# Local attention and a feed-forward layer: a tile of 128 queries split into two of 64 with 120 keys each

## The chip, the core and the metric

The kernel runs on one NeuronCore of a Trainium2 chip. The engines are TensorE (matmuls, written PE; its loads of the stationary operand are listed apart as PEld), VectorE (DVE), ScalarE (ACT), GpSimd (POOL) and SyncE (SP), which issues the DMAs. The metric is the device time of one execution in microseconds (us); lower is better.

## The reference

The attention of 4 batches of 768 tokens with 8 heads of 64 is followed by a feed-forward layer. Each query sees the keys closer than 16 positions to its own, and beside them 24 summary keys, one for each block of 32 tokens (the maximum of the block's keys, with the mean of its values):

```python
block, window = (32, 16)
nb = S // block                                   # 24
k_sum = k.reshape(B, H, nb, block, D).max(axis=3)
v_sum = v.reshape(B, H, nb, block, D).mean(axis=3)
mask_l = np.abs(pos[:, None] - pos[None, :]) < window
scores_s = scale * np.einsum('bhsd,bhnd->bhsn', q, k_sum) + np.log(block)
scores_all = np.concatenate([np.where(mask_l, scale * q @ k^T, -1e9), scores_s], axis=-1)
a = softmax(scores_all)
attn = np.matmul(a, np.concatenate([v, v_sum], axis=2))
# feed-forward on x = attn as (3072, 512)
h = x @ w_in                                      # (512, 2048)
out = (h * sigmoid(h)) @ w_out                    # (2048, 512)
```

Everything is f32. The time goes mostly into the feed-forward products.

## The kernel before

**Stages.** The 3072 tokens are 24 stages of 128 queries (`s`; six to a batch). A stage handles its 8 heads in four groups of two (`m = 4 s + g`). A query tile needs its own 128 keys, 15 on either side (the side block, 30 of 32 places) and the 24 summary keys: `NKEY` = 128 + 32 + 24 = 184.

**A head group (`job_a`).** TensorE multiplies queries and keys (L555; one block of instructions serves two head groups; the 64 rows of one head and the 64 of another are used side by side and write two PSUM banks). VectorE adds the mask and takes the maximum (L561), ScalarE makes the exponential and its sum (L564), VectorE the reciprocal (L568, L569), and one of three engines scales (L574, L576, L578). In batch 0 all this is f32: TensorE transposes the weights, the 128 own keys (L587) and the 56 others (L589), copies bring them back (L225, L229), and the products with v are f32 too (L619), a main block of 128 rows and a side block of 56. In batches 1 to 3 operands are split into a high and a low f16 part. The scores are three products (high by high, low by high, high by low), VectorE makes the low part of the weights (L602, four operations a head group), a DMA transposes them (L605), and the products with v (`job_c`, L634) are five terms for each of 8 heads, 40 matmuls of 128 columns a stage, two heads side by side in the two halves of the array's columns.

**v.** `job_mean` loads the six v tiles of batch 0 (L483), and a matmul with a matrix of 1/32 (`blocks`, L485) sums them into the 24 means. `job_vs` loads the side block (L501) and copies the means below it. `job_scale0` takes the maxima of v (L492). The two places for these tiles that lie in the weight buffers `wr` are given to the last weights later.

**Feed-forward (`job_f`).** Chunks of 256 tokens; for each of 16 slices of the hidden layer, L727 (chunk 0, f32) or L730 (f16, 12 matmuls) makes h, ScalarE the tanh (L744), VectorE the product (L745), and L735 or L738 multiplies by w_out. The weights are loaded in 32 pieces of 512 KB (L660), decoded by ScalarE and VectorE (L674, L670, L676), measured (L677) and after a common scale (`w_scale`) split (L683, L685). Chunk 0 uses them in f32, before the scale is known. It needs x of stages 0 and 1, which is copied by L225 and L229.

**Order.** Every operation is told to a planner (`Plan.op`) with a cost for each engine that may do it, its reads and writes, and a priority from the table `TUNE`. The planner fixes engine and order in advance; every engine then runs its instructions in that order. Where it sees TensorE wait early, it puts fillers (L316, L722), matmuls without use for the result. All loads go through SyncE's one queue.

Of the kernel before, what the change touches and what calls it, by code (L numbers as in the profile page):

```python
# [20 lines left out]
DM, DFF = 512, 2048  # L21
# [7 lines left out]
NSIDE = BLK  # L29
NLOC = P + NSIDE  # L30
NKEY = NLOC + NB
NS2 = NSIDE + NB
UW = 3 * P
# [4 lines left out]
NSTG = NT // P  # L38
NPAIR = NSTG * 4
# [179 lines left out]
def local_attn_ffn(ctx: ExitStack, tc: tile.TileContext, qkT, qF, kF, v, vR, w, out):  # L219
# [27 lines left out]
    blocks = const.tile([P, 11 * 4], F32, name="blocks")  # L247
    nc.vector.memset(blocks, 0.0)
    for j in range(4):
        nc.vector.memset(blocks[j * BLK:(j + 1) * BLK, 20 + j:21 + j], 1.0 / BLK)  # L250
# [3 lines left out]
    nc.vector.memset(masks[:, :, :NLOC], 0.0)  # L254
    nc.vector.memset(masks[:, :, NLOC:], math.log(BLK) / ISQ)
    for i in range(3):
        m = masks[:, i, :]
        nc.gpsimd.affine_select(out=m[:, :P], in_=m[:, :P], pattern=[[-1, P]], compare_op=ALU.is_ge, fill=NEG, base=HALO, channel_multiplier=1)
        nc.gpsimd.affine_select(out=m[:, :P], in_=m[:, :P], pattern=[[1, P]], compare_op=ALU.is_ge, fill=NEG, base=HALO, channel_multiplier=-1)
        if i == 0:  # L260
            nc.vector.memset(m[:, P:P + HALO], NEG)
        else:
            nc.gpsimd.affine_select(out=m[:, P:P + HALO], in_=m[:, P:P + HALO], pattern=[[1, HALO]], compare_op=ALU.is_ge, fill=NEG, base=0, channel_multiplier=-1)
        if i == 2:
            nc.vector.memset(m[:, P + HALO:NLOC], NEG)
# [7 lines left out]
    first = const.tile([P, max(NP * 2 * UW + 8 * DM, NTILE * 8 * NKEY)], F16, name="first")  # L273
    second = const.tile([P, 2 * max(8 * QW + 8 * NB, (NQ0 + NS0) * DM)], F16, name="second")
# [61 lines left out]
    def nudge(tag, *at):  # L336
        return NUDGE.get("_".join((tag,) + tuple(str(x) for x in at)), 0.0)
# [570 lines left out]
```

## Time and profile before

| | |
|---|---|
| median of 3 runs | 634.98 us (634.79 to 636.36) |
| the profiled execution | 634.78 us, its span 633.0 us |
| busy: PE, DVE, ACT, POOL | 625.0, 498.6, 400.7, 86.3 us |
| granted TensorE clock | 0.999 |
| DMA | 79.63 MB, 126 GB/s over the span |

The span is the time from the first to the last instruction of the program; 1.8 us lie around it. Busy time of TensorE counts overlapping matmuls once. A line of the timeline has start, length, engine, line of the code, operation, output and inputs, shape and count; a shape such as `128*64 128x128` is rows by columns of the stationary operand, and the moving operand. An f32 matmul stands as two records. A block is a run of matmuls of one line; its cost is the time from its start to the start of the block behind it, which contains the change of shape.

### The profile page before, as it was taken

How to read it: one execution, taken by the hardware profiler on the slowest of the kernel's cores; microseconds unless marked ns; L12 is line 12 of the kernel's file. 1: busy time of each engine (PE TensorE's matmuls, PEld its weight loads, DVE VectorE, ACT ScalarE, POOL GpSimd, SP SyncE). 2: the span in 40 equal slices, each digit the busy share in tenths (PEclk: the TensorE clock that was granted, in tenths of full speed). 3: DMA queues.
4: the chain of work that ended last, by engine and by line, in shares of the span. 5: the costliest groups of instructions: out<-in, count | busy, mean ns of one | idle time of the engine just before them, and what ended most of it. 6: DMA issues, size and time to landing. Idle time of an engine off the chain costs nothing.

```text
span 633.0 us, 13973 instructions
## 1 busy us (share of the span) xinstructions
PE 625.0 (99%) x5001; PEld 415.3 (66%) x5001; DVE 498.6 (79%) x1656; ACT 400.7 (63%) x1072; POOL 86.3 (14%) x125
## 2 busy tenths in 40 slices
PE   7999999999999999999999999999999999999997
PEld 4566666666666666666666666676666666666664
DVE  6899979977899785997989984998897968843332
ACT  3899969864885674665757674665765556533333
POOL 2311000130434100101003100001114104000000
PEclk9999999999999999999999999999999999999999
DMA  8999151222543593562553772454451523310000
GB/s 271 357 415 364 28 183 59 93 60 71 175 106 94 154 215 103 141 148 76 149 119 42 195 215 85 109 144 112 140 117 45 164 50 48 87 28 1 35 0 35
DMA packets 84455, 79.63 MB, mean 126 GB/s; under 512 B 60416, under 2 KB 66560, under 8 KB 84384
## 3 DMA queue, kind: packets, MB, share of 16 engines
q1 hardware_dynamic: 84384, 78.73, 44.0%
q8 instruction: 39, 0.64, 0.4%
q14 instruction: 32, 0.26, 0.1%
HBM read 56.49 MB, written 6.29 MB: 99 GB/s over the span
## 4 chain that ended last, share of the span: by engine, by line
PE 85%; DMA 5%; DVE 4%; ACT 3%; SPq 1%; issue 1%; ACTq 0%
PE bank L730 37%; PE bank L738 37%; PE bank L555 4%; DMA wr<-in_w_dram 4%; PE bank L634 4%; DVE wm L677 1%; PE bank L735 1%; DVE wr L676 1%; PE bank L619 1%; ACT wr L674 1%; ACT wr L670 1%; SPq L354 1%; DMA wr<-in_v_dram 1%; DMA raw<-in_qF_dram 1%; PE bank L727 1%
## 5 line engine op out<-in xcount | busy, mean ns | idle before, releaser
L730 PE MATMUL bank<-x,wr 128*128 128x256 f16 x2112 | 258.7, 273 | 0.0
L730 PEld LDWEIGHTS <-wr 128*128 128x128 f16 x2112 | 205.2, 98 | 57.0 <-issue 2.3
L738 PE MATMUL bank<-wr,gh 128*128 128x512 f16 x704 | 209.8, 380 | 0.0
L744 ACT ACTIVATE t<-bank,th 128x256 f32<-128x256 f32 x176 | 82.7, 470 | 119.2 <-PE bank L730 118.9
L745 DVE SCALAR_TENSOR_TENSOR t<-t,bank 128x256 f32<-128x256 f32 x192 | 79.5, 415 | 72.8 <-ACT t L744 72.0
L738 PE MATMUL bank<-wr,gl 128*128 128x512 f16 x352 | 133.4, 379 | 0.0
L747 ACT ACTIVATE gh<-t 128x256 f16<-128x256 f32 x176 | 72.3, 413 | 67.8 <-DVE t L745 60.1
L748 DVE SCALAR_TENSOR_TENSOR gl<-t,gh 128x256 f16<-128x256 f32 x176 | 80.8, 460 | 29.3 <-ACT gh L747 28.7
L738 PEld LDWEIGHTS <-gh 128*128 128x128 f16 x704 | 65.3, 98 | 48.2 <-issue 3.8
L564 ACT ACTIVATE e<-e,mx 128x184 f32<-128x184 f32 x192 | 83.5, 436 | 5.9 <-DVE mx L561 5.7
L602 DVE SCALAR_TENSOR_TENSOR first<-e,sum,first 128x128 f16<-128x128 f32 (+1 forms) x288 | 78.6, 333 | 0.3 <-POOL first L576 0.3
L738 PEld LDWEIGHTS <-gl 128*128 128x128 f16 x352 | 34.4, 98 | 41.6 <-DVE gl L748 0.2
L561 DVE CUSTOM_DVE_ANT_0 e<-bank,masks,qsc 128x184 f32<-128x184 f32 x144 | 52.1, 401 | 2.5 <-PE bank L555 2.5
L564 ACT ACTIVATION_READ_ACCUMULATOR e<-e,mx 128x1 f32 x192 | 36.2, 189 | 0.0
L576 POOL TENSOR_SCALAR first<-e,sum 128x184 f16<-128x184 f32 x27 | 13.4, 499 | 149.9 <-DVE sum L569 76.8
L735 PE MATMUL bank<-wr,t 128*128 128x512 f32 x64 | 31.0, 602 | 0.0
L727 PE MATMUL bank<-x,wr 128*128 128x256 f32 x128 | 30.3, 381 | 0.2 <-DVE t L745 0.2
L727 PEld LDWEIGHTS bank<-x,wr 128*128 128x128 f32 x128 | 24.1, 190 | 9.1 <-issue 4.8
L232 POOL TENSOR_TENSOR first<-raw,first 128x1024 f16<-128x1024 f32 x12 | 27.0, 2251 | 10.8 <-ACT first L225 10.0
L576 POOL TENSOR_SCALAR e<-e,sum 128x184 f32<-128x184 f32 x28 | 12.6, 456 | 102.3 <-DVE sum L568 61.2
L578 DVE TENSOR_SCALAR first<-e,sum 128x184 f16<-128x184 f32 x76 | 24.5, 352 | 0.6
L634 PEld LDWEIGHTS <-first 128*64 128x64 f16 x720 | 20.6, 110 | 6.0 <-issue 6.0
(146 smaller groups left out, 676.5 us busy)
## 6 DMA issues: line engine op xcount, KB each, us to landing
wr<-in_w_dram SPq DMA_DIRECT2D x32, 512.0 KB
raw<-in_qkT_dram SPq DMA_DIRECT2D x18, 576.0 KB
raw<-in_v_dram SPq DMA_DIRECT2D x18, 512.0 KB
out_dram<-raw SPq DMA_DIRECT2D x24, 256.0 KB
raw<-in_kF_dram SPq DMA_DIRECT2D x12, 384.0 KB
raw<-in_qF_dram SPq DMA_DIRECT2D x9, 512.0 KB
raw<-in_vR_dram SPq DMA_DIRECT2D x12, 384.0 KB
first<-in_qkT_dram SPq DMA_DIRECT2D x6, 320.0 KB
```

Source lines behind the costliest of these rows:

```text
L561: plan.op({"dve": 326 if b else 270}, lambda e, i=i: nc.vector.tensor_tensor_reduce(out=et[:, i, :], in0=sc[:, i, :NKEY], in1=mask, scale= ...
L564: plan.op({"act": 431}, lambda e, i=i: nc.scalar.activation(out=et[:, i, :], in_=et[:, i, :], func=AF.Exp, scale=-1.0, bias=mx[:, i:i + 1] ...
L602: nc.vector.scalar_tensor_tensor(out=pt[:, i, to:to + z - a], in0=et[:, i, a:z], scalar=su[:, i:i + 1], in1=pt[:, i, a:z], op0=ALU.mult, o ...
L634: nc.tensor.matmul(out=av[j * D:(j + 1) * D, i * P:(i + 1) * P], lhsT=vt[:, vi, h * D:(h + 1) * D], rhs=tt[:, j * 3 + blk, :], start=(n == ...
L727: nc.tensor.matmul(out=h, lhsT=wi.bitcast(F32)[:, ct * P:(ct + 1) * P], rhs=x0[:, ct, :], start=(ct == 0), stop=(ct == NCT - 1))
L730: nc.tensor.matmul(out=h, lhsT=wip[:, part, ct * P:(ct + 1) * P], rhs=x[:, ct, :], start=(ct == 0 and q == 0), stop=(ct == NCT - 1 and q = ...
L735: nc.tensor.matmul(out=bank[ob[u]], lhsT=t[:, u * P:u * P + P], rhs=wo.bitcast(F32), start=opens, stop=closes)
L738: nc.tensor.matmul(out=bank[ob[u]], lhsT=g[:, u * P:u * P + P], rhs=wop[:, part, :], start=(opens and q == 0), stop=(closes and q == 2))
L744: plan.op({"act": 264 if c == 0 else 360}, lambda e: nc.scalar.activation(out=t, in_=h, func=AF.Tanh, scale=0.5 if c == 0 else th[:, 0:1]) ...
L745: plan.op({"dve": 337}, lambda e: nc.vector.scalar_tensor_tensor(out=t, in0=t, scalar=1.0, in1=h, op0=ALU.add, op1=ALU.mult), r=[("bank", ...
L747: plan.op({"act": 311}, lambda e: nc.scalar.activation(out=gh, in_=t, func=AF.Copy, scale=SHRINK), r=[("t", j)], w=[("gh", n)], prio=post)
L748: plan.op({"dve": 343}, lambda e: nc.vector.scalar_tensor_tensor(out=gl, in0=t, scalar=SHRINK, in1=gh, op0=ALU.mult, op1=ALU.subtract), r= ...
```

## The change

The tile of 128 queries becomes two of 64 (`z` = 0, 1). Each has 64 own keys, 32 places for both sides (15 + 15 + 2 unused) and 24 summary keys: `NKEY` is now 64 + 32 + 24 = 120, at most 128, so that there is one contraction block and no side block. The summary keys stand at both ends of the stored key tile, so that either half finds its 120 keys in one piece.

```diff
-NSIDE = BLK
-NLOC = P + NSIDE
-NKEY = NLOC + NB
-UW = 3 * P
+HALF = P // 2
+NLOC = P + 2 * HALO + 2
+NKEY = HALF + BLK + NB
+OFF = HALF + NB
+KT = NLOC + 2 * NB
+UW = 2 * P
...
-    NRAW, NP, NTT, NE, NG, NT2 = 3, 4, 8, 3, 4, 4
-    NPT, NQ0, NS0 = 6, 2, 3
+    NRAW, NP, NTT, NE, NG, NT2 = 3, 8, 12, 3, 4, 4
+    NQ0 = 4
...
 # summary keys to both ends of the key tile (batch 0; the same for batches 1 to 3)
-copy(e, k0_t[t][:, :, NLOC:], km_t[0])
+copy(e, both_ends(k0_t[t]), to_ends(km_t[0]))
...
 # scores (job_a)
                 for n in range(3 if b else 1):
-                    for u in range(2):
-                        rows = slice(u * 64, u * 64 + 64)
...
-                        nc.tensor.matmul(out=bank[both[u]][:, i * 256:i * 256 + NKEY], lhsT=q, rhs=kk, start=(n == 0), stop=(n == (2 if b else 0)))
+                    for z in range(2):
+                        for u in range(2):
+                            rows = slice(u * 64, u * 64 + 64)
...
+                            nc.tensor.matmul(out=bank[both[u]][side[z], i * 256:i * 256 + NKEY], lhsT=q[:, side[z]], rhs=kk[:, z * OFF:z * OFF + NKEY], start=(n == 0), stop=(n == (2 if b else 0)))
...
 # batch 0: transposes, and one copy for two
                 for i in range(2):
-                    nc.tensor.transpose(out=tp[:, i, :], in_=et[:, i, :P], identity=ident)
-                for i in range(2):
-                    nc.tensor.transpose(out=tp[:NS2, 2 + i, :], in_=et[:, i, P:], identity=ident)
+                    nc.tensor.transpose(out=tp[:NKEY, i, :], in_=et[:, i, :], identity=ident)
...
 # batches 1 to 3: low part of the weights
-                for to, a, z in ((2 * P, 0, P), (P + 64, P, NKEY)):
-                    nc.vector.scalar_tensor_tensor(out=pt[:, i, to:to + z - a], in0=et[:, i, a:z], scalar=su[:, i:i + 1], in1=pt[:, i, a:z], op0=ALU.mult, op1=ALU.subtract)
+                nc.vector.scalar_tensor_tensor(out=pt[:, i, P:P + NKEY], in0=et[:, i, :], scalar=su[:, i:i + 1], in1=pt[:, i, :NKEY], op0=ALU.mult, op1=ALU.subtract)
...
 # products with v, batch 0 (job_c)
-                for blk in range(2):
+                for z in range(2):
                     for j in range(2):
-                        rows = slice(0, P if blk == 0 else NS2)
-                        nc.tensor.matmul(out=av[j * D:(j + 1) * D, g * P:(g + 1) * P], lhsT=(side if blk else vm)[rows, (2 * g + j) * D:(2 * g + j + 1) * D], rhs=tt[rows, 2 * blk + j, :], start=(blk == 0), stop=(blk == 1))
+                        nc.tensor.matmul(out=av[j * D:(j + 1) * D, g * P + z * HALF:g * P + z * HALF + HALF], lhsT=src[:NKEY, z, (2 * g + j) * D:(2 * g + j + 1) * D], rhs=tt[:NKEY, j, side[z]], start=True, stop=True)
...
 # products with v, batches 1 to 3
-        terms = ((v1, 0, 0), (v2, 0, 0), (v1, 1, 1), (v2, 1, 1), (v1, 0, 2))
...
-                for n, (vt, vi, blk) in enumerate(terms):
-                    for j in range(2):
-                        h = 2 * i + j
-                        nc.tensor.matmul(out=av[j * D:(j + 1) * D, i * P:(i + 1) * P], lhsT=vt[:, vi, h * D:(h + 1) * D], rhs=tt[:, j * 3 + blk, :], start=(n == 0), stop=(n == 4))
+                for z in range(2):
+                    for n, (vt, part) in enumerate(((v1, 0), (v2, 0), (v1, 1))):
+                        for j in range(2):
+                            h = 2 * i + j
+                            nc.tensor.matmul(out=av[j * D:(j + 1) * D, i * P + z * HALF:i * P + z * HALF + HALF], lhsT=vt[:NKEY, z, h * D:(h + 1) * D], rhs=tt[:NKEY, 2 * j + part, side[z]], start=(n == 0), stop=(n == 2))
...
 # v of batch 0 (job_mean): two pieces a tile, a matmul each, and the means copied into both
+            for z in range(2):
+                plan.op({"dma": 650}, lambda e, src=src, t=t, z=z: nc.sync.dma_start(out=src[rows0[z], z], in_=v[0, t, rows0[z], z, :]), w=[keys[z]], prio=prio)
...
+                plan.op({"pe": 900}, lambda e, src=src, t=t, z=z, at=at, k=k: nc.tensor.matmul(out=bank[k][:NB], lhsT=sums[rows0[z], z, at:at + NB], rhs=src[rows0[z], z], start=(t == 0 and z == 0), stop=(t == NTILE - 1 and z == 1)),
...
+                plan.op({"pool": 742, "act": 560, "dve": 335}, lambda e, src=src, z=z: copy(e, src[rowsm[z], z], mean), r=["vms"], w=[mkeys[z]], prio=when(4 * t))
...
 # maxima of v (job_scale0): both pieces in one operation
-nc.vector.tensor_reduce(out=am_t[:, t:t + 1], in_=src, ...)
+nc.vector.tensor_reduce(out=am_t[:NKEY, t:t + 1], in_=src[:NKEY].rearrange("p a c -> p (a c)"), ...)
```

The masks are built anew for the two halves, the host lays v and the keys out to match, the costs told to the planner follow the new sizes, and all numbers of `TUNE` are other ones, so that the order changes everywhere. TensorE has 49 fillers of L316 before and 60 after.

On TensorE, this stands before from the first scores to the first products with v (batch 0, stage 0; `first` and `second` hold keys and queries, `e` the weights, `wr` and `v` the value tiles; each f32 matmul is one row or one count here):

```order
L555 MATMUL bank_199<-first,second 128x184
L555 MATMUL bank_200<-first,second 128x184
...
L485 MATMUL bank_203<-wr,blocks 24x512
L587 MATMUL bank_199<-ident,e_180 128x128 x2
L589 MATMUL bank_199<-ident,e_180 56x128 x2
L485 MATMUL bank_203<-v_154,blocks 24x512
L485 MATMUL bank_203<-v_155,blocks 24x512
L409 MATMUL bank_203<-ident,am 1x128
L619 MATMUL bank_204<-third,wr 64x128 x2
L619 MATMUL bank_204<-third,second 64x128 x2
```

And after:

```order
L577 MATMUL bank_207<-first,second 64x120
L577 MATMUL bank_208<-first,second 64x120
...
L504 MATMUL bank_211<-wr,sums 24x512 x3
L609 MATMUL bank_207<-ident,e_188 120x128 x2
L504 MATMUL bank_211<-v_161,sums 24x512 x2
L504 MATMUL bank_211<-v_162,sums 24x512
L609 MATMUL bank_209<-ident,e_188 120x128 x2
L316 LDWEIGHTS ident
L316 MATMUL bank_205<-ident 128x256
L636 MATMUL bank_212<-third,wr 64x64 x16
```

The scores of stage 1 and all twelve matmuls of the means now come ahead of the first products of stage 0, fillers stand between, and the 16 products of a stage follow one another.

On SyncE, this is the start of the queue before (`first` and `second` receive keys and queries of batch 0, `wr` first v and then weights):

```order
L354 DMA first<-in_qkT_dram 128x4x160 x6
L455 DMA second<-in_qkT_dram 128x4x128
L483 DMA wr<-in_v_dram 128x512 x4
L483 DMA v_154<-in_v_dram 128x512
L483 DMA v_155<-in_v_dram 128x512
L501 DMA second<-in_v_dram 32x512 x2
L660 DMA wr<-in_w_dram 128x1024 x4
L501 DMA second<-in_v_dram 32x512
L660 DMA wr<-in_w_dram 128x1024 x5
```

And after:

```order
L362 DMA first<-in_qkT_dram 128x4x160 x6
L464 DMA second<-in_qkT_dram 128x4x128
L499 DMA wr<-in_v_dram 120x512
L499 DMA wr<-in_v_dram 96x512
...
L499 DMA v_162<-in_v_dram 120x512
L499 DMA v_162<-in_v_dram 96x512
L677 DMA wr<-in_w_dram 128x1024
L353 DMA raw_156<-in_kF_dram 128x768
L677 DMA wr<-in_w_dram 128x1024 x6
```

All of v now goes ahead of the first weight, the side loads between the weights are gone, and one load for batch 1 (L353) comes forward among them.

More of the change, by code (lines that the diff above doesn't have):

```diff
@@ L245, in local_attn_ffn @@
     nc.vector.memset(ones, 1.0)
[L247 to L250, printed above, removed]
+    sums = const.tile([P, 2, NB + 4 * NTILE - 2], F32, name="sums")
+    nc.vector.memset(sums, 0.0)
+    for z in range(2):
+        two, top = sums[:, z, NB - 2:NB], HALO + (0 if z else NB)
+        nc.vector.memset(two, 1.0 / BLK)
+        nc.gpsimd.affine_select(out=two, in_=two, pattern=[[-BLK, 2]], compare_op=ALU.is_ge, fill=0.0, base=-top, channel_multiplier=1)
+        nc.gpsimd.affine_select(out=two, in_=two, pattern=[[BLK, 2]], compare_op=ALU.is_ge, fill=0.0, base=top + BLK - 1, channel_multiplier=-1)
     lg = const.tile([P, 1], F32, name="lg")
@@ L270, in local_attn_ffn @@
-    NRAW, NP, NTT, NE, NG, NT2 = 3, 4, 8, 3, 4, 4
-    NPT, NQ0, NS0 = 6, 2, 3
+    side = [slice(z * HALF, z * HALF + HALF) for z in range(2)]
+    local = [slice(NB, NKEY), slice(0, NKEY - NB)]
+    means = [slice(0, NB), slice(NKEY - NB, NKEY)]
+    nc.vector.memset(masks, 0.0)
+    for z in range(2):
+        nc.vector.memset(masks[side[z], :, means[z]], math.log(BLK) / ISQ)
+        for i in range(3):
+            m = masks[side[z], i, local[z]]
+            n = NKEY - NB
+            nc.gpsimd.affine_select(out=m, in_=m, pattern=[[1, n]], compare_op=ALU.is_ge, fill=NEG, base=0, channel_multiplier=-1)
+            nc.gpsimd.affine_select(out=m, in_=m, pattern=[[-1, n]], compare_op=ALU.is_ge, fill=NEG, base=2 * HALO, channel_multiplier=1)
@@ L272, in local_attn_ffn @@
+    nc.vector.memset(masks[side[0], 0, NB:NB + HALO], NEG)
+    nc.vector.memset(masks[side[1], 2, HALF + HALO:NKEY - NB], NEG)
+    NRAW, NP, NTT, NE, NG, NT2 = 3, 8, 12, 3, 4, 4
+    NQ0 = 4
     raw = ring(NRAW, [P, 4 * QW], F32, "raw")
-    first = const.tile([P, max(NP * 2 * UW + 8 * DM, NTILE * 8 * NKEY)], F16, name="first")
-    second = const.tile([P, 2 * max(8 * QW + 8 * NB, (NQ0 + NS0) * DM)], F16, name="second")
-    third = const.tile([P, NTT * 6 * P], F16, name="third")
+    first = const.tile([P, max(NP * 2 * UW + 8 * DM, NTILE * 8 * KT)], F16, name="first")
@@ L276, in local_attn_ffn @@
+    half = 8 * P + 8 * KT
+    second = const.tile([P, 2 * max(half, NQ0 * DM)], F16, name="second")
+    third = const.tile([P, NTT * 4 * P], F16, name="third")
     p_t = [first[:, i * 2 * UW:(i + 1) * 2 * UW].rearrange("p (a b) -> p a b", a=2) for i in range(NP)]
@@ L499, in job_vs @@
         if b == 0:
-            side, i = s0_t[s % NS0], s % NS0
-            plan.op({"dma": 650}, lambda e: nc.sync.dma_start(out=side[:NSIDE], in_=v[0, t, :NSIDE, 1, :]), w=[("s0", i)], prio=prio)
-            plan.op({"pool": 742, "act": 560, "dve": 335}, lambda e: copy(e, side[NSIDE:NS2], mean), r=["vms"], w=[("s0m", i)], prio=prio)
             return
@@ L509, in vm @@
         def vm(e):
-            for u in range(2):
-                nc.sync.dma_start(out=vr[u * 64 + NSIDE:u * 64 + NS2, 1, :], in_=mean)
+            for z in range(2):
+                nc.sync.dma_start(out=vr[rowsm[z], z, :], in_=mean)
         plan.op({"dma": 1400}, vm, r=["vms"], w=key, prio=prio)
@@ L779, in job_stage @@
                 release("first", [(x, i) for x in ("k0", "k0m") for i in range(NTILE)], p[0] - TUNE["qk"])
-                release("second", [("q0", i) for i in range(NQ0)] + [(x, i) for x in ("s0", "s0m") for i in range(NS0)], p[0] - TUNE["qk"])
-                release("third", [("pt", i) for i in range(NPT)] + [("pt", i, "side") for i in range(NPT)], p[0] - TUNE["qk"])
+                release("second", [("q0", i) for i in range(NQ0)], p[0] - TUNE["qk"])
+                release("third", [("pt", i) for i in range(NTT)], p[0] - TUNE["qk"])
                 for i in range(NP):
```

137 lines of the change are left out of this document (66 added, 71 removed).

## Prediction

> **What bounds the kernel now.** I read the page first (busy shares), then the stretches of the span, then the matmuls one block at a time.
>
> ```profile
> PE 625.0 (99%) x5001; PEld 415.3 (66%) x5001; DVE 498.6 (79%) x1656; ACT 400.7 (63%) x1072; POOL 86.3 (14%) x125
> PEclk9999999999999999999999999999999999999999
> ```
> ```profile
> 11.05:33.27 22.22, 22.15 (x160) 11.38 (x161) 18.75 (x80) 19.04 (x61) 7.20 (x16) 1.00 0.99 353
> 33.27:103.86 70.59, 69.73 (x319) 44.57 (x319) 65.67 (x162) 63.73 (x147) 4.73 (x9) 1.00 0.56 213
> 144.50:568.00 423.50, 423.50 (x3748) 285.73 (x3747) 352.57 (x1235) 262.39 (x725) 63.60 (x69) 1.00 0.47 117
> ```
> The columns are stretch, length, busy PE, PEld, DVE, ACT, POOL, granted clock, DMA share, GB/s. From 144.5 to 568 us, where batches 1 to 3 are attended between feed-forward blocks, TensorE never stops, while VectorE is busy 352.57 of 423.5 us and ScalarE 262.39. The granted clock is 1.00. So there TensorE's own work is the time, and what the change takes off it comes off the end. Before 103.86 us TensorE is just as full, but the 16 DMA engines (0.99), ScalarE and VectorE are nearly full as well; there a saving on TensorE may run into something else. All sums are made against the profiled execution, 634.78 us with a span of 633.0; it lies 0.2 us under the median of 634.98.
>
> **The change part by part.** The price of a matmul comes from blocks: the start of a block to the start of the next.
>
> ```profile
> 81.20 1.19 DVE wm L677 x2
> ...
> 103.86 1.31 PE bank L730 x12
> 105.17 0.82 PE bank L555 x8
> ```
> ```profile
> L634 PE MATMUL bank<-third,first 128*64 128x128 f16 x720 | 23.5, 220 | 0.0
> L634 PEld LDWEIGHTS <-first 128*64 128x64 f16 x720 | 20.6, 110 | 6.0 <-issue 6.0
> ```
> ```profile
> 187.67 1.31 PE L634 MATMUL bank<-third,first 128*64 128x128 f16 x40
> 188.91 0.61 PE L738 MATMUL bank<-wr,gh 128*128 128x512 f16 x2
> 188.59 0.39 PE L634 MATMUL bank<-third,first 128*64 128x128 f16 x8
> ```
> Twelve f16 matmuls of 256 columns (L730, in the chain of waits) take 1.31 us: 0.426 ns a column. A product block (L634) of 40 matmuls takes 188.91 - 187.67 = 1.24 us. Its matmuls run two at a time, one in each half of the array's columns: one lasts 0.22 us, so in the last row the first of 8 starts 0.39 - 0.22 = 0.17 us before the last, three steps of 0.056 us, which is 128 columns at 0.426 plus 0.002. So 20 steps are 1.11 us, and 0.13 us is the change of shape around the block.
>
> *Products, batches 1 to 3.* 40 matmuls of 128 columns become 48 of 64, still two at a time: 24 steps of 0.027 + 0.002 = 0.029 us, 0.70 us, with the 0.13 us unchanged 0.83 us. 0.41 us saved in each of 18 stages: 7.4 us.
>
> No row shows a step of 64 columns, and the loads of the stationary operand must keep up with it:
>
> ```profile
> 187.67 0.14 PEld L634 LDWEIGHTS <-first 128*64 128x64 f16 x4 [0.21 <-issue]
> 302.79 0.12 PEld L555 LDWEIGHTS <-second 64*128 64x128 f16 x4 [0.21 <-issue]
> ```
> A load lasts 0.11 us in L634, and four, two to each half, stand in 0.14: the second load of a half starts 0.03 us after the first. A step of 0.056 us is the moving columns alone, so the 0.03 us load runs beside the matmul before it. The Trainium skill ("TensorE: Matmul & The Clock Gate", part 3, what overlaps and what doesn't) says a load overlaps running matmuls only in another row group. Both halves of L634 use all 128 rows, so by that rule its step would be 0.056 + 0.03 = 0.086 us; the trace disagrees, and I follow the trace. By the rule a new step would cost 0.059 us and the block 1.55, and this term would turn from -7.4 into +5.6 us.
>
> *Scores, batches 1 to 3.*
> ```profile
> 302.79 0.65 PE L555 MATMUL bank<-second 64*128 64x184 f16 x12
> 303.37 0.60 PE L738 MATMUL bank<-wr,gh 128*128 128x512 f16 x2
> ```
> 0.58 us for 6 steps of two: 184 columns are 0.078 us, 6 steps 0.47, the rest 0.11. After: 24 matmuls in 6 steps of four, 120 columns each, 0.052 us: 0.31 + 0.11 = 0.42. 0.16 us saved in 36 blocks: 5.8 us. The 0.03 us load hides under 0.052. Two row halves at once (L555) and two column halves at once (L634) are each shown; four quarters are not. The bounds are 6 steps and 12 steps of 0.052.
>
> *Batch 0, all f32 (a matmul is two records).*
> ```profile
> 66.32 1.88 PE L735 MATMUL bank<-wr,t 128*128 128x512 f32 x4
> 68.04 1.89 PE L727 MATMUL bank<-x,wr 128*128 128x256 f32 x8
> 69.86 0.89 PE L555 MATMUL bank<-first,second 64*128 64x184 f32 x8
> 70.68 1.98 PE L735 MATMUL bank<-wr,t 128*128 128x512 f32 x4
> 75.95 0.40 PE L587 MATMUL bank<-ident,e 128*128 128x128 f32 x2
> 76.18 0.38 PE L589 MATMUL bank<-ident,e 128*56 128x128 f32 x2
> 76.40 0.38 PE L587 MATMUL bank<-ident,e 128*128 128x128 f32 x2
> 62.53 0.44 PE L619 MATMUL bank<-third,second 56*64 56x128 f32 x4
> 62.90 0.44 PE L619 MATMUL bank<-third,wr 128*64 128x128 f32 x4
> 63.27 0.44 PE L619 MATMUL bank<-third,second 56*64 56x128 f32 x4
> 13.67 1.90 PE L485 MATMUL bank<-wr,blocks 128*24 128x512 f32 x4
> 15.50 0.44 PE L587 MATMUL bank<-ident,e 128*128 128x128 f32 x2
> ```
> The rate is 1.72 us for 4 records of 512: 0.84 ns a column. Scores: 0.82 us, 4 steps of 0.155 and 0.20 of shape and load; after 4 steps of 120 columns, 0.101: 0.60. 0.22 x 12 blocks = 2.6 us. Transposes: 4 of 0.11 us a head group become 2: 0.22 x 24 = 5.2 us. Products (L619): each group of four records takes 0.37 us, two steps of 0.108 and 0.15 because the main block of 128 keys and the side block of 56 alternate; two groups are 0.74. After, 8 records of one shape: 4 steps of 0.054 and 0.15 once, 0.37. 0.37 x 24 = 8.8 us. Means of v (L485): 15.50 - 13.67 = 1.83 us for two matmuls; 6 become 12, +0.915 x 6 = 5.5 us. Sum of batch 0: -11.1 us.
>
> TensorE loses 7.4 + 5.8 + 11.1 = 24.3 us. Of batch 0, stages 4 and 5 (8 x 0.59 + 4 x 0.22 = 5.6 us) run after 103.86 (their first scores at 105.17) among full feed-forward blocks and count in full; the other 5.5 us lie before it.
>
> *What else moves before 104 us.*
> ```profile
> wr<-in_v_dram SPq DMA_DIRECT2D x4, 256.0 KB
> second<-in_v_dram SPq DMA_DIRECT2D x6, 64.0 KB
> ```
> ```profile
> 32.54 0.68 DVE L229 COPY x<-bank 128x512 f32<-128x512 f32 x1
> 33.27 3.72 PE L727 MATMUL bank<-x,wr 128*128 128x256 f32 x16
> 15.84 0.68 DVE L492 TENSOR_REDUCE am<-v 128x1 f32<-128x512 f32 x1
> 20.31 1.30 POOL L227 TENSOR_SCALAR second<-vms 24x512 f32<-24x512 f32 x2 [1.36 <-ACT vms L225]
> ```
> The six v loads of 256 KB and six of 64 KB become twelve of 240 and 192 KB, all ahead of the first weight in SyncE's queue, one q tile less: 672 KB, at 353 GB/s 1.9 us later for the first weight. SyncE issues twelve either way. But what starts the feed-forward at 33.27 us is not a weight: it is the copy of x that ends at 33.22. What it follows is attention of stages 0 and 1, in which the 5.5 us of extra means eat what scores, transposes and products save (8 x 0.59 + 4 x 0.22 = 5.6). Twelve copies of the mean rows (0.65 us on POOL) replace six, and now stand ahead of every product of their stage; they are spread over POOL and ScalarE. The six maxima of v double in width, at most +0.68 us each, 4.1 us on VectorE, and move behind the scores; against that the second copy of each transposed tile goes. So I take the start of the feed-forward as unchanged, and TensorE's 5.6 us of stages 2 and 3 as the saving between 33 and 104, where VectorE (65.67 of 70.59) leaves little room. The order adds 11 fillers to TensorE there, places where it would wait. Bounds of this early part: -5.5 us (all of it) and +3 us (first weight late, VectorE late). I take -3.9, nearer the full saving, as TensorE is full in the rows, and the last weight's maximum (L677, the last step of decoding) is done at 82.4 us, 21 us before TensorE ends this part.
>
> Off the path: VectorE's four low-part operations a head group become two, and scores and exponentials are 120 wide instead of 184. With VectorE at 83% this gives nothing, but keeps it off the path when the stretch shortens. POOL's wider copies of the key maxima cost nothing: POOL is busy 63.60 of 423.5 us.
>
> Sum: 7.4 + 5.8 + 5.6 + 3.9 = 22.7 us; 634.8 - 22.7 = **612 us**.
>
> **Rivals.**
> *The early part gives nothing back or loses 3 us* (weights and VectorE bound it): 634.8 - 18.8 = 616, to 619. For it: DMA 0.99 to 33 us. Chance 0.14.
>
> *Four quarters run only two at a time.* Scores then take 12 steps: 0.73 us, +0.15 x 36 = 5.6 instead of -5.8; f32 8 steps, 1.01 us, +2.3 instead of -2.6. Worth +16.3: about 628. Against it: each pairing alone runs. Chance 0.07.
>
> *A floor per matmul, low or high.* The forecast needs a product matmul with its load every 0.029 / 2 = 14.5 ns and a score matmul every 13. The densest stretch in the trace is 40 in 1.11 us, 28 ns each; nothing shows TensorE fed faster for long. Against a floor for each instruction:
> ```profile
> 187.67 0.25 PE L634 MATMUL bank<-third,first 128*64 128x128 f16 x2
> ```
> two matmuls of at least 0.22 us stand within 0.25, so different halves start close together. Scores and products of batches 1 to 3 become 864 + 864 matmuls, so each ns of floor costs 1.7 us. At 21 ns, half way, products are 48 x 0.021 + 0.13 = 1.14 us and scores 24 x 0.021 + 0.11 = 0.61: 612 + 5.6 + 7.0 = 625. At 28 ns products are 1.47 (+4.2 us) and scores 0.78 (+7.2); with batch 0 (its scores 0.65, the rest as before: -10.6, less the 1.6 lost early) that is 637. This rival ends on the slower side from 27 ns on; at 31 ns (1.24 us over 40) it is 642. Chance 0.07 below 27 ns, 0.06 above. The Trainium skill (same page, part 1, on the 2.5 ns floor) says start to start never falls under about 25 ns however few the columns; by that, products would be 1.33 us, scores 0.71, and the time 632. The row of two within 0.25 us disagrees for different halves; no row here has a matmul under 128 columns in one half.
>
> *Loads add to matmuls instead of running beside them.* Products 24 x (0.029 + 0.03) + 0.13 = 1.55 us (+5.6), scores +0.7, batch 0 -3.5 with the 1.6 lost: about 639. The steps of 0.056 speak against it. Chance 0.02.
>
> **How the numbers follow.** My forecast has 0.62 and its own range 606 to 618. The smaller gains (616 to 619, 628, 625) are faster too: 0.90 in all. Within 0.3% (1.9 us, about what a measurement of this kernel can tell from no change) 0.04; slower 0.06. The range of 8 in 10 is 604 to 628.
>
> **What would show it.** Right: product blocks near 0.83 us and score blocks near 0.42 us between the same neighbours; transposes of 0.22 and products of 0.37 a head group in batch 0; the first L730 block (a new line number) between 98 and 102 us; TensorE full from there to the end. Wrong: blocks that grow with the number of matmuls, not columns; gaps of TensorE between 20 and 40 us; a first f16 block after 104 us; or TensorE waiting in the middle because VectorE's order, not its load, is late.

## The result, and the profile after

| | before | after |
|---|---|---|
| median | 635.60 us (634.79 to 636.36, 4 runs) | 617.03 us (616.10 to 617.71, 4 runs) |
| ratio, 95% interval | | 0.9707 (0.9685 to 0.9729) |
| profiled execution | 634.78 us, span 633.0 | 616.48 us, span 614.4 |
| first matmul of chunk 0 (L727, now L744) | 33.27 us | 37.08 us |
| first f16 feed-forward block (L730, now L747) | 103.70 us | 101.14 us |

The change saves 18.6 us, 2.9%. The forecast was 22.7 us and 612 us; the time lies inside the forecast's own range of 606 to 618, near its upper end and 5 us above the point. The f16 block of before starts at 103.70 us; 103.86 in the prediction is where the chain of waits passes on to the same block. Most line numbers moved with the change. In after, scores stand in L577, transposes L609, products L636 (batch 0) and L651, means of v L504, copies L224 (ScalarE), L226 (POOL) and L228 (VectorE).

The page of after, busy shares and granted clock:

```profile
PE 603.8 (98%) x5648; PEld 398.1 (65%) x5648; DVE 462.7 (75%) x1517; ACT 380.3 (62%) x1049; POOL 97.1 (16%) x136
PEclk9999999999999999999999999999999999999999
```

TensorE runs 647 matmul records more than before (5001) and is busy 21 us less. The three stretches that answer to those of before (stretch, length, busy PE, PEld, DVE, ACT, POOL, granted clock, DMA share, GB/s), cut at the first feed-forward matmul and the first f16 block:

```profile
11.00:37.08 26.08, 23.89 (x207) 10.10 (x207) 17.72 (x77) 20.37 (x70) 8.74 (x18) 0.93 1.05 324
37.08:101.14 64.06, 64.06 (x323) 41.26 (x324) 61.43 (x152) 56.18 (x130) 2.49 (x7) 1.00 0.61 232
144.50:550.00 405.50, 404.47 (x4277) 271.66 (x4276) 317.76 (x1104) 242.85 (x697) 74.39 (x74) 1.00 0.43 110
```

The second and third stretches look as before: TensorE full, at the full clock. The first does not: TensorE stands still for over 2 us of 26, and the granted clock is 0.93. The middle stretch, from the first feed-forward matmul to the first f16 block, was 70.4 us and is 64.06. So there are three accounts: the start is 3.8 us later, the stretch behind it 6.4 us shorter, and from the first f16 block to the end 513.3 us stand where 529.3 stood, 16.0 less. The sum is -18.6.

The price of the new blocks, in the timeline of TensorE (start, length, engine, line, operation, tiles, shape, count):

```profile
48.16 0.38 PE L609 MATMUL bank<-ident,e 128*120 128x128 f32 x2
48.37 1.02 PE L752 MATMUL bank<-wr,t 128*128 128x512 f32 x2
...
50.98 0.45 PE L636 MATMUL bank<-third,wr 120*64 120x64 f32 x8
51.37 0.64 PE L577 MATMUL bank<-first,second 64*64 64x120 f32 x16
51.94 1.99 PE L744 MATMUL bank<-x,wr 128*128 128x256 f32 x8
...
259.84 0.51 PE L577 MATMUL bank<-second 64*64 64x120 f16 x24
260.28 1.48 PE L747 MATMUL bank<-x,wr 128*128 128x256 f16 x12
...
268.75 0.95 PE L651 MATMUL bank<-third,first 120*64 120x64 f16 x48
269.63 0.28 PE L747 MATMUL bank<-x,wr 128*128 128x256 f16 x1
```

From start to next start: the two transposes of a head group of batch 0 cost 0.21 us, its products 0.39, f32 scores 0.57, f16 scores 0.44 and a product block 0.88 us. The forecasts were 0.22, 0.37, 0.60, 0.42 and 0.83.

The chain of work that ends with the first feed-forward matmul (start, length, engine, line):

```profile
27.63 0.98 PE bank L504 x2
...
28.63 0.58 ACT vms L224
...
29.63 1.14 ACT wr L224 x2
...
31.43 1.62 ACT e L586 x8
...
34.76 0.68 ACT wr L691
35.44 0.56 ACT e L596 x2
36.00 0.57 ACT wr L687
36.57 0.47 ACT x L224
37.04 0.04 issue
37.08 3.07 PE bank L744 x13
```

Before, TensorE's last matmul for the means, and ScalarE's copy of their sum, stood here:

```profile
18.50 1.04 PE L485 MATMUL bank<-v,blocks 128*24 128x512 f32 x2
...
19.58 0.57 ACT L225 COPY vms<-bank 24x512 f32<-24x512 f32 x1
```

So the means are complete at 28.6 instead of about 19.5 us, and behind them ScalarE does, in its fixed order, the copy of the sum (`vms`), copies of it into the value tiles, exponentials, two steps of the decoding of weights (L691, L687) and only then the copy of x that the feed-forward waits for. Of these 9 us, about 5.4 are the six additional matmuls (0.9 us each) and 1.7 a lower clock (see e12); the rest is not broken down. From `vms` to the first feed-forward matmul there are 8.45 us, where before there were 13.69 (19.58 to 33.27); so 9.05 us later and 5.24 us shorter make the 3.8.

One wait is left behind 37 us, at 188.6. The waits of TensorE from there to the end and the chain around it:

```profile
PE bank L651 <- DVE x L668: 1.0, 1, 1.0
```
```profile
186.52 2.44 DVE second L474
188.96 0.61 DVE x L668
189.57 0.04 issue
189.61 0.95 PE bank L651 x48
```

VectorE does L474 for 2.44 us ahead of the operation on x (L668, its low part) that frees the bank. That is not the usual length of L474; the second row is what POOL does meanwhile:

```profile
L474 DVE TENSOR_SCALAR second<-raw,qsc x4: 477/481/2439, 172.4 to 300.0; 128x512 f16<-128x512 f32 x4
186.55 2.13 POOL L231 TENSOR_TENSOR first<-raw,first 128x1024 f16<-128x1024 f32 x1
```

The other three of L474 took 0.48 us, and no POOL operation ran beside them; this one lasts until L231 of POOL is done. The 2 us that it is too long are more than the wait, so neither VectorE's load nor its order alone makes the wait. That POOL is the reason was not tried by a run.

### The profile page after: what moved, and what is told of

Same layout as the page of the kernel before. It is cut to its first block, busy times and chain, and to the rows that moved or that the text cites. A ratio compares the mean times of both kernels' runs of the same rounds, so it can differ in the third digit from the quotient of the medians.

```text
span 614.4 us, 15092 instructions
## 1 busy us (share of the span) xinstructions
PE 603.8 (98%) x5648; PEld 398.1 (65%) x5648; DVE 462.7 (75%) x1517; ACT 380.3 (62%) x1049; POOL 97.1 (16%) x136
## 4 chain that ended last, share of the span: by engine, by line
PE 95%; ACT 2%; SPq 1%; DVE 1%; DMA 1%; issue 0%
PE bank L747 38%; PE bank L755 38%; PE bank L744 5%; PE bank L752 5%; PE bank L577 4%; PE bank L651 2%; PE bank L504 2%; PE bank L636 1%; PE bank L609 1%; DMA wr<-in_v_dram 1%; SPq L362 1%; ACT wr L224 0%; DVE second L474 0%; ACT e L586 0%; PE bank L451 0%; PE bank L430 0%
## 5 line engine op out<-in xcount | busy, mean ns | idle before, releaser
L747 PE MATMUL bank<-x,wr 128*128 128x256 f16 x2112 | 258.1, 273 | 0.0
L747 PEld LDWEIGHTS <-wr 128*128 128x128 f16 x2112 | 204.8, 98 | 55.7 <-issue 0.9
L586 ACT ACTIVATE e<-e,mx 128x120 f32<-128x120 f32 x192 | 73.3, 386 | 4.6 <-DVE mx L583 4.0
L620 DVE SCALAR_TENSOR_TENSOR first<-e,sum,first 128x120 f16<-128x120 f32 x144 | 47.7, 377 | 0.1
L583 DVE CUSTOM_DVE_ANT_0 e<-bank,masks,qsc 128x120 f32<-128x120 f32 x144 | 41.7, 337 | 0.3 <-PE bank L577 0.3
L744 PE MATMUL bank<-x,wr 128*128 128x256 f32 x128 | 30.6, 383 | 0.3 <-ACT x L224 0.3
L744 PEld LDWEIGHTS bank<-x,wr 128*128 128x128 f32 x128 | 23.8, 190 | 7.7 <-issue 3.3
L231 POOL TENSOR_TENSOR first<-raw,first 128x1024 f16<-128x1024 f32 x13 | 28.2, 2174 | 0.9
L598 POOL TENSOR_SCALAR e<-e,sum 128x120 f32<-128x120 f32 x24 | 10.1, 427 | 111.3 <-DVE sum L591 103.1
L598 POOL TENSOR_SCALAR first<-e,sum 128x120 f16<-128x120 f32 x26 | 13.5, 522 | 82.2 <-DVE sum L591 40.5
L226 POOL TENSOR_SCALAR first<-raw 128x1024 f16<-128x1024 f32 x12 | 14.1, 1176 | 77.5 <-PE bank L651 77.3
L600 DVE TENSOR_SCALAR first<-e,sum 128x120 f16<-128x120 f32 x91 | 23.8, 288 | 0.8
```

What stands on the lines that cost most here:

```text
L231: eng[e].tensor_tensor(out=out, in0=in0, in1=in1, op=ALU.subtract)
L583: plan.op({"dve": 262 if b else 206}, lambda e, i=i: nc.vector.tensor_tensor_reduce(out=et[:, i, :], in0=sc[:, i, :NKEY], in1=mask, scale= ...
L586: plan.op({"act": 385}, lambda e, i=i: nc.scalar.activation(out=et[:, i, :], in_=et[:, i, :], func=AF.Exp, scale=-1.0, bias=mx[:, i:i + 1] ...
L620: nc.vector.scalar_tensor_tensor(out=pt[:, i, P:P + NKEY], in0=et[:, i, :], scalar=su[:, i:i + 1], in1=pt[:, i, :NKEY], op0=ALU.mult, op1= ...
L744: nc.tensor.matmul(out=h, lhsT=wi.bitcast(F32)[:, ct * P:(ct + 1) * P], rhs=x0[:, ct, :], start=(ct == 0), stop=(ct == NCT - 1))
L747: nc.tensor.matmul(out=h, lhsT=wip[:, part, ct * P:(ct + 1) * P], rhs=x[:, ct, :], start=(ct == 0 and q == 0), stop=(ct == NCT - 1 and q = ...
```

## The experiments

All twelve are listed, one kernel each, beside runs of before on the same chip. "Start" is the first matmul of chunk 0, "f16" the first f16 feed-forward block, both of the profiled execution.

| run | median us (range) | ratio, 95% interval | start | f16 |
|---|---|---|---|---|
| after | 617.03 (616.10 to 617.71) | 0.9707 (0.9685 to 0.9729) | 37.08 | 101.14 |
| e1_mean6 | 619.14 (618.30 to 619.54) | 0.9735 (0.9720 to 0.9749) | 38.95 | 103.01 |
| e2_clock | 617.81 (617.04 to 619.60) | 0.9723 (0.9700 to 0.9746) | 37.87 | 101.92 |
| e3_v_whole | 615.78 (614.68 to 616.60) | 0.9682 (0.9664 to 0.9701) | 36.74 | 100.80 |
| e4_low4 | 617.49 (617.08 to 618.45) | 0.9713 (0.9697 to 0.9728) | 38.33 | 102.39 |
| e5_whole_mean6 | 615.67 (614.39 to 616.18) | 0.9673 (0.9656 to 0.9690) | 34.02 | 98.08 |
| e6_best | 617.92 (617.23 to 618.67) | 0.9714 (0.9695 to 0.9734) | 35.12 | 103.12 |
| e7_z_outer | 617.64 (617.09 to 618.32) | 0.9707 (0.9692 to 0.9723) | 37.20 | 101.26 |
| e8_prod_32 | 617.57 (616.73 to 618.15) | 0.9705 (0.9688 to 0.9721) | 38.75 | 102.81 |
| e9_prod_32x32 | 615.27 (614.54 to 617.76) | 0.9686 (0.9664 to 0.9707) | 38.08 | 102.14 |
| e10_v_128rows | 616.32 (615.92 to 617.60) | 0.9699 (0.9680 to 0.9718) | 36.93 | 100.98 |
| e11_best2 | 624.13 (621.95 to 625.44) | 0.9813 (0.9791 to 0.9835) | 36.09 | 101.06 |
| e12_whole_clock | 614.74 (614.39 to 614.88) | 0.9671 (0.9656 to 0.9686) | 35.29 | 99.35 |

In all but e6 and e11 the distance from start to f16 is 64.06 us, as in after: what moves the start moves the rest with it. The start itself moves by 1.7 us between kernels that differ in nothing ahead of it (after 37.08, e9 38.08, e8 38.75), so for the early part the chain and the waits say more than the time. From `vms` to the start there are 8.4 to 8.5 us in every run but e1 (8.7) and e11 (8.0), so what moves the start lies ahead of `vms`. In the kernels with nothing different there it goes with ScalarE's wait for a weight: 0.7 us in after, 1.1 in e7 (start 37.20), 2.0 in e9, 2.3 in e8 and 2.9 in e4 (38.33, with the clock at 1.00).

**Why does the feed-forward start late? The means alone.**

```diff
-... lhsT=sums[rows0[z], z, at:at + NB], rhs=src[rows0[z], z], start=(t == 0 and z == 0), ...
+None if z else ... start=(t == 0), ...
```

> The changed kernel without the six matmuls that sum the second half of each v tile (the means are then incomplete); loads, copies and order as they are. Theory A (the early gain was eaten on TensorE: twelve matmuls of 0.91 us for the means instead of six stand ahead of the first products): the feed-forward starts about 5 us earlier than 37.1 us, the first f16 block comes 3 to 5 us before 101.1, and the time is 612 to 614 us. Theory B (from 33 to 100 us VectorE and ScalarE set the pace, so an earlier start gives nothing): first f16 block near 101, 617 us.

The start came at 38.95, later than in after. The last of the remaining matmuls for the means ended at 24.4 us, but TensorE then stood for 4.2 us, and the copy `vms` came at 30.2. Waits between 20 and 37 us (engine, line, what for: us in total, times, longest):

```profile
PE bank L609 <- ACT e L596: 4.6, 2, 4.2
ACT wr L691 <- DMA wr<-in_w_dram: 3.9, 1, 3.9
```

ScalarE waited for a weight, and the scaling (L596) that TensorE's transposes need stands behind the decoding of that weight (L691) in its order. The theory that the means alone set the start fell.

**The clock alone.** Between 11 and 20 us the granted clock was 0.81 in after; the first three f32 matmuls of L504 (six records) took 4.4 us.

```diff
+            if e == "pe" and not opened:
+                fills, opened = fills + 20, True
```

> The changed kernel with 20 more fillers on TensorE ahead of its first scores, so that it doesn't wait 2.7 us at 8.7 us. Theory A' (the granted clock fell to 0.5 for 3.4 us after that wait and made the first three means 4.36 us instead of 2.7): clock 1.00 from 12 to 20 us, the feed-forward starts 1.0 to 1.7 us earlier, time 615.5 to 616.3. Theory B: the clock holds but the first f16 block stays at 101 us, 617.

The clock stayed at 1.00, and the start did not move forward (37.87). The same wait as in e1 took the gain:

```profile
ACT wr L693 <- DMA wr<-in_w_dram: 3.0, 1, 3.0
```

**The loads of v alone.** SyncE's one queue carries v ahead of the first weights.

```diff
-... nc.sync.dma_start(out=src[rows0[z], z], in_=v[0, t, rows0[z], z, :]), ...   # twelve, 120 or 96 rows of 2 KB
+... nc.sync.dma_start(out=src, in_=v[0, t]) if z == 0 else None, ...            # six, 128 rows of 4 KB
```

> The changed kernel with six loads of 128 rows of 4 KB for v of batch 0 instead of twelve of 120 or 96 rows of 2 KB; the queue's order is kept. Theory A (TensorE's own matmuls are the early limit, it has no gap from 12 to 29 us): packets and landing are faster, the feed-forward starts within 1 us of 37.1, 616 to 617.5. Theory C (v arrives late because its packets took 0.13 us instead of 0.09, and the means wait for it): the feed-forward starts 3 to 5 us earlier, time 613 to 615.

and, to tell the number of rows from the size of a packet, twelve loads with `src[:, z]` and `v[0, t, :, z, :]`, 128 rows of 2 KB:

> The twelve loads of v as in the changed kernel, in 2 KB packets, but each of all 128 rows instead of 120 and 96. Theory A (rows that do not divide evenly over the 16 DMA engines make the packets slow): packets at 85 to 90 ns as before the change, over 320 GB/s between 11 and 20 us (241 in the changed kernel), the time 615.5 to 617. Theory B (packets of 2 KB are slow in this place whatever the rows): packets stay over 125 ns and the rate under 280 GB/s, the time 617 to 618.

The stretch from 11 to 20 us in after, in e3 and in e10, one fence each:

```profile
11.00:20.00 9.00, 8.46 (x54) 2.61 (x58) 3.73 (x27) 5.51 (x24) 2.09 (x6) 0.81 1.06 241
```
```profile
11.00:20.00 9.00, 8.67 (x64) 3.00 (x64) 3.87 (x27) 5.63 (x24) 2.14 (x6) 0.81 1.03 390
```
```profile
11.00:20.00 9.00, 8.57 (x60) 2.78 (x64) 3.93 (x27) 5.71 (x24) 2.15 (x6) 0.81 1.06 379
```

The DMA share is full in all three, but the last column is 241, 390 and 379 GB/s. The packets of e10 are as small as those of after, so it is the loads of 120 and 96 rows that are slow here. With either edit ScalarE no longer waits for a weight. Yet the start moved only 0.2 to 0.3 us: now the means on TensorE bind, in which e3 and e10 still have the slow clock.

**Both at once.**

> Both early chains are shortened at once: v is loaded in six whole loads of 128 x 1024 (4 KB a packet), and six of the twelve matmuls that sum v into means are left out, so half of each v tile is missing in the means. Theory A (two chains of nearly equal length, the means on TensorE and the arrival of the first weights, set the start of the feed-forward; cutting one alone gains nothing): the first feed-forward matmul starts at about 33 to 34 us (37.1 in the changed kernel, 36.7 with whole loads alone, 38.9 with half of the means alone), the first f16 block between 97 and 98.5, the time 612.5 to 614. Theory B (VectorE and ScalarE, full between 33 and 100 us, or the weights that come later, set the end of the early part): the start moves, but the first f16 block stays at 100.5 to 101.2, the time 615.5 to 617.

```profile
33.50 0.47 ACT x L224
...
34.02 3.72 PE bank L744 x16
```

The start came at 34.02 and the f16 block at 98.08, as the theory of two chains has it (33 to 34, 97 to 98.5); VectorE and ScalarE did not hold the middle stretch back. The profiled execution took 614.39 us; the median of 615.67 lies above the 614 expected. Part of the gain is the clock, which stayed at 1.00 in this run.

> Nothing left out: whole loads of v (the weights come early) and 20 more fillers on TensorE at its first wait, so that the granted clock does not fall while the first means are summed (with whole loads alone it was 0.81 between 11 and 20 us, and the first six matmuls of the means took 4.4 instead of 2.7 us). Theory A (two chains of nearly equal length; with the weights early, the means on TensorE bind, so the 1.7 us of the slow clock now count, though with late weights they did not): the feed-forward starts at 34.9 to 35.6 us (36.7 with whole loads alone), the first f16 block at 99 to 99.7, the time 614 to 615.3. Theory B (with whole loads the start is set by weights and their decoding, not by TensorE): start 36.4 to 37, first f16 block 100.5 to 101, the time 615.5 to 616.5.

```profile
12.48 2.74 PE bank L506 x6
...
26.84 0.58 ACT vms L226
...
35.29 3.72 PE bank L746 x16
```

Whole loads and fillers leave nothing out. The first three matmuls of the means (six records) took 2.74 instead of 4.42 us, the means were complete at 26.8 instead of 28.6, and the start came at 35.29: 1.45 us before e3, where the clock alone (e2) had gained nothing. So two chains of nearly equal length end at the start: the means (TensorE, then ScalarE's copies) and v, then the first weights, in SyncE's queue. Its five runs, 614.39 to 614.88, lie below all four of after. But the runs of before that stand beside them are faster too (median 635.08 for 635.60), and the intervals of the two ratios just touch (0.9656 to 0.9686 and 0.9685 to 0.9729). So this version clearly beats before; a gain of about 2 us over after is likely, not shown.

**Copies and maxima out of the way.** Two tries to move what ScalarE and VectorE do ahead of the copy of x.

```diff
+... r=["vms"] + ([("xh", 0, 1)] if i > 1 else []), ...      # copies of the means, stages 2 to 5
+... r=keys + mkeys + [("xh", 0, 1)], ...                    # maxima of v
```

> Nothing left out. Whole loads of v, 20 more fillers on TensorE at the start, and the copies of the means for stages 2 to 5 and the maxima of v are made to wait until x of stage 1 is copied, so that on ScalarE and VectorE they no longer stand ahead of it. Theory A (these copies and maxima in the fixed order hold up the copy of x, as the chain of the changed kernel reads): the feed-forward starts at 33.5 to 35 us, the first f16 block at 98 to 99.5, the time 613 to 614.5. Theory B (the arrival and decoding of the first weight sets the start, which 20 fillers and the copies cannot change): start 36.5 to 37, the time 615.5 to 617, as with whole loads alone.

```profile
35.10 4.58 DVE L513 TENSOR_REDUCE am<-wr 120x1 f32<-120x1024 f32 x4
35.12 3.72 PE L745 MATMUL bank<-x,wr 128*128 128x256 f32 x16
39.61 2.33 DVE L513 TENSOR_REDUCE am<-v 120x1 f32<-120x1024 f32 x2
42.26 0.31 PE L420 MATMUL bank<-ident,am 128*1 128x128 f32 x1 [2.81 <-DMA wr<-in_w_dram]
```

The start came at 35.12, at the edge of what was expected. But the six maxima (L513), 1.16 us each, now stand together on VectorE, and TensorE waits 2.81 us for the last of them (L420 transposes the result; the DMA named had long been done). The f16 block came at 103.1, 2 us later than in after. Against e12, from which e6 differs in nothing else, the start moved by 0.17 us only, and from `vms` to it there are still 8.4 us: in the places of the copies ScalarE does more of the decoding of weights (L692, five times between 30.99 and 35.09).

> Nothing left out: whole loads of v, the copies of the means for stages 2 to 5 and the maxima of v behind the copy of x of stage 1, no additional fillers, and the priority of the maxima set 214 later, so that they are spread between the steps of chunk 0 instead of standing back to back ahead of its first one, where they cost TensorE 2.81 us. Theory A (the place of these operations in VectorE's and ScalarE's order sets the start, and the earlier start is kept if they do not stand together): the feed-forward starts at 34 to 35.5 us, no wait over 1 us between 37 and 60, the first f16 block at 98 to 100, the time 613 to 615. Theory B (VectorE, busy 22 of 23 us between 37 and 60, has no room for the 7 us of maxima there): the start comes early but TensorE loses it again between 37 and 60, first f16 block at 101 or later, the time 616 to 618.

With the maxima spread there was no wait over 1 us between 37 and 60, but the start was 36.09, outside what was expected, and the f16 block at 101.06. Neither theory gave the 624 us: the planner laid the whole order anew, and TensorE met new waits behind it (6.9 us in all from 37 us on, about 1 in after), of which these are the longest:

```profile
PE bank L578 <- DVE mx L584: 2.7, 1, 2.7
PE bank L610 <- ACT e L597: 1.4, 1, 1.4
```

What these copies and maxima cost in place is therefore not settled; both ways of moving them cost more than they gave.

**VectorE's relief.** The low part of the weights in four operations a head group again (more instructions for the same work):

```diff
-nc.vector.scalar_tensor_tensor(out=pt[:, i, P:P + NKEY], in0=et[:, i, :], ...)
+for a, z in ((0, 64), (64, NKEY)):
+    nc.vector.scalar_tensor_tensor(out=pt[:, i, P + a:P + z], in0=et[:, i, a:z], ...)
```

> The changed kernel with each low-part operation of VectorE cut in two (64 and 56 wide), so that a head group has four again; 144 more operations of about 0.3 us, 40 us of VectorE work back, order and the rest as they are. If TensorE alone sets the time after 101 us (VectorE's relief is off the path): 617 to 618 us, TensorE without gaps. Rival (part of the gain came from VectorE's relief): 622 us or more.

```profile
144.50:550.00 405.50, 404.08 (x4272) 271.30 (x4271) 332.41 (x1250) 243.31 (x698) 75.04 (x74) 1.00 0.41 110
```

VectorE is busy 14.7 us more in this stretch, TensorE the same; the one wait grew from 1.03 to 1.42 us, and the ratio is that of after. The 40 us that were expected back on VectorE did not come, but its share of the stretch is 82%, as much as before the change (83%; 78% in after). The relief is worth nothing, as forecast.

**What sets a score step?** The order of the 24 matmuls in a block changed so that neighbours share a half of the columns:

```diff
-for n in range(3 if b else 1):
-    for z in range(2):
+for z in range(2):
+    for n in range(3 if b else 1):
```

> The same score matmuls in another order: all of query half 0 of a head pair, then all of query half 1, so that two neighbours in the instruction stream fall in one half of the array's columns and only two, not four, can run side by side. Theory A (scores go four quarters at once, a step is the 120 columns): the f16 score blocks grow from 0.44 us to 0.73 to 0.80, the f32 ones from 0.57 to about 1.0, the time by 36 x 0.31 + 12 x 0.2 = 11 to 14 us, to 628 to 631. Theory B (a matmul costs its instruction, about 13 ns, whatever its neighbours): blocks unchanged, the time 617.

```profile
260.11 0.52 PE L577 MATMUL bank<-second 64*64 64x120 f16 x24
260.57 0.39 PE L747 MATMUL bank<-x,wr 128*128 128x256 f16 x2
```

The block is 0.455 instead of 0.442 us. (Only these f16 blocks are reordered: in batch 0 `n` has one value, so the f32 part of the expectation could not be tested.) But this doesn't favour a price per instruction either: in after four matmuls start within 0.010 us and the next four 0.053 us after them, where a price for each instruction would spread them evenly. 24 matmuls of 120 columns at 0.426 ns are 1.23 us of columns, and two at a time they would need 0.61; the first and the last start lie 0.30 us apart in after and 0.31 here. So four quarters run at once in this order too. In the trace the two further quarters start 0.020 us after the first two, once in a block, and then keep that distance; that is the 0.013 us. A matmul of the second half of the columns thus starts ahead of older ones that wait for their quarter. The Trainium skill ("TensorE: Matmul & The Clock Gate", part 3, what overlaps and what doesn't) says that matmuls start strictly in order; by that this order would need 9 steps at the least, as only the last step of one half of the columns can be shared with the first of the other. With 0.052 us a step and 0.13 around them that would be 0.60 us a block, an estimate, and this run does not bear it out for separate quarters.

**What sets a product step?** In after a step of two product matmuls is 31.7 ns (the starts lie between 0.052 and 0.749 us of the block, 22 steps), 2.7 more than forecast.

```diff
-out=av[..., i * P + z * HALF:i * P + z * HALF + HALF], ..., rhs=tt[:NKEY, 2 * j + part, side[z]]
+out=av[..., i * P + z * HALF:i * P + z * HALF + 32], ..., rhs=tt[:NKEY, 2 * j + part, z * HALF:z * HALF + 32]
```

> The products of batches 1 to 3 use 32 moving columns instead of 64, so half of the queries of these batches get no output; the number of matmuls and loads stays. A step of two matmuls took 31.4 ns where 29 were forecast. Theory A (a step is its columns and 2 to 4 ns): 15.5 to 18 ns, the block falls from 0.88 to 0.50 to 0.55 us, the time by 18 x 0.35 = 6.3 us, to 611. Theory B (the loads of the stationary operand, two halves of 64 columns each a step, or the issue of instructions have become the limit at 31 ns): blocks stay at 0.85 to 0.88 us, the time 616.5 to 617.

```profile
270.51 0.93 PE L651 MATMUL bank<-third,first 120*64 120x32 f16 x48
271.38 0.28 PE L747 MATMUL bank<-x,wr 128*128 128x256 f16 x1
```

Half of the moving columns, and the block is 0.87 instead of 0.88 us, the step 31.6 ns: it is not the columns. Then the stationary operand was halved as well (`lhsT=vt[:NKEY, z, h * D:h * D + 32]`):

> As the run with 32 moving columns, but the stationary operand is 32 columns wide too, so three quarters of the output of batches 1 to 3 are left out; 48 matmuls and 48 loads as before. With 64 stationary columns the block stayed at 0.87 us whether 64 or 32 columns moved. Theory A (the load of 64 stationary columns takes about 27 to 31 ns and, within one half of the array, stands between two matmuls; it sets the step): 32 columns take about half, the step of two falls from 31 to 16 to 18 ns, the block to 0.50 to 0.56 us, the time by 6 us, to 611. Theory B (a fixed cost for each matmul with its load, about 15.7 ns): block 0.85 to 0.87 us, the time 617.

```profile
269.43 0.77 PE L651 MATMUL bank<-third,first 120*32 120x32 f16 x48
270.13 0.39 PE L747 MATMUL bank<-x,wr 128*128 128x256 f16 x2
```

The block is 0.70 us, the step 25.0 ns, between the 16 to 18 and the 31 of the two theories. So the width of the load counts (6.6 ns for 32 columns), but something else keeps the step at 25 ns, for 32 columns need 13.6. The loads alone do not make it either. At the start of a block, where no load waits for a matmul, the first four loads, two to each half, stand like this in after and in e9:

```profile
268.74 0.14 PEld L651 LDWEIGHTS <-first 120*64 120x64 f16 x4 [0.42 <-issue]
```
```profile
269.43 0.11 PEld L651 LDWEIGHTS <-first 120*32 120x32 f16 x4 [0.42 <-issue]
```

In the traces the second load of a half starts 0.028 us after the first with 64 columns and 0.015 with 32, both less than the step. The Trainium skill (same page, part 1, on the 2.5 ns) says that start to start never falls under about 25 ns. For the stream as a whole that doesn't hold: in after a product matmul starts every 15.8 ns, here every 12.5. For each half of the array by itself the trace agrees, with 25.0 ns here. What sets 31.7 ns at 64 stationary columns, and 25.0 at 32, was not tried further.

## Why the prediction was right, and where it was off

The time alone does not show that the forecast was right: 617 us also lies in the range of the first rival (616 to 619), in which the early part gives nothing or loses. The stretches decide between them: the early part gave 2.6 us, and TensorE's own work gave the rest.

- **Scores, batches 1 to 3 (-5.8 us).** Four quarters side by side: shown. Block 0.442 instead of 0.42: -5.0 us. The step of 0.052 was right; 0.13 instead of 0.11 us stand around it.
- **Products, batches 1 to 3 (-7.4).** 0.881 instead of 0.83: -6.5 us. The mis-sized term is the step, 0.0317 for 0.029. The sentence that failed is that a 64-column step is its columns and that the load is hidden: e8 and e9 show that at this size the step goes by the width of the stationary operand and not by the moving columns. The prediction's own row had the load at 0.03 us, no shorter than the 0.029 that it took for the step. The load does overlap the matmul ahead of it (else 0.059), so the rival with added loads fell, and so did the floors of 21 and 28 ns, with a matmul every 15.8 ns. The row of two matmuls within 0.25 us, which the prediction set against a floor of 25 ns, does not contradict it: it allows starts 0.03 us apart.
- **Batch 0 (-11.1).** Stages 4 and 5, 5.6 us: scores 0.57 (0.60), transposes as forecast, products 0.38 to 0.39 (0.37). With these, the last stretch adds up: 6.5 + 5.0 + 5.6 less the one wait of 1.0 is 16.1, and 16.0 were measured. A wait in the middle was listed among the signs of a wrong forecast, with VectorE's order as its reason; it came and is worth 1.0 us, but behind it stands one operation five times as long as its like. Gaps of TensorE between 20 and 40 us, another sign, came too (0.8, 0.5 and 0.3 us).
- **The early part (-3.9, bounds -5.5 to +3).** Its sum came out at -2.6 by two errors against each other; that it lies so near -3.9 is luck. "I take the start of the feed-forward as unchanged" failed: it is 3.8 us later. Behind it the saving was 6.4, more than the full 5.6: I held back nearly a third because VectorE was nearly full, and e5 shows that it didn't bind. The 0.8 beyond 5.6 are waits of TensorE that the stretch had before (69.73 busy of 70.59 us) and has no more (64.06 of 64.06). The failed step is that the means' extra 5.5 us are eaten by what scores and transposes save. That is a sum of TensorE's time; but all products of stage 0 and 1 wait for the *last* mean, and that came 9 us later (28.6 for 19.5), with a row of ScalarE's work of 8.45 us behind it. That TensorE's clock would fall stood in no term, and a late first weight only in the bound of +3. The v loads I priced by their bytes at 353 GB/s; with 120 and 96 rows they ran at 241.
- **VectorE's relief worth nothing:** shown (e4).

In all: 3.8 late at the start, 2.5 better behind it, 0.9 + 0.8 for the blocks and 1.0 for the wait make 4.0 of the 4.1 us between 22.7 and 18.6.

## What to carry to other kernels

Price narrower matmuls by the moving columns and by the load of the stationary operand, and measure the step where the two are close; here 64 columns against 64 stationary ones had already passed the point where fewer columns give anything (31.7 against 31.6 ns), and halving both gave 25.0, not half. When work ahead of a join is split, follow the item that finishes last through the fixed order of every engine behind it; a sum over the engine that is full does not show a join. Where two chains of about equal length end at one point, cutting one alone gives next to nothing (e1 and e2 for the means, e3 and e10 for the loads), so cut both (e5, e12) before calling one harmless. Before a wait is put down to an engine's order, compare the length of the operation ahead of it with that of its like.

## What the runs showed of the hardware

- Loads of 120 and 96 rows with 2 KB a row ran at 241 GB/s where 128 rows of the same 2 KB ran at 379, at a full DMA share both times. Why was not found.
- The clock: TensorE's wait of 2.38 us at about 9 us (e4), and shorter ones (before 2.08), left the granted clock at 1.00; at the same place waits of 2.67 us and more (e9, after, e3) were followed by a lower one, 0.81 as the mean from 11 to 20 us in after. The length of the wait alone does not decide: one of 2.72 us at 160 us in e11 left the clock at 1.00. The lower clock cost 1.45 us at the start where the path leads over TensorE (e12 against e3, one profile each), and nothing where the weights came last (e2).
- Quarters of the array take their matmuls independently: the order in the instruction stream, within a block of 24, moved the block by 0.013 us.
- A VectorE operation can be several times longer than its like while POOL works: L474 took 2.44 us beside POOL's L231 of 2.13 us, and 0.48 us three times without it (after). In e4 it is L621 ahead of the same wait, four in 3.34 us instead of 0.85. Not every VectorE operation beside L231 was long, and why was not tried.
